# One searched instruction order replaced by another in a retention and channel-mix kernel

## The chip, the cores and the metric

One core of one Trainium2 chip. The metric is device time in microseconds of the one launch. A second number, the span, is the time from the first to the last instruction of one profiled execution.

## The reference

Two steps. First a retention recurrence over 4 sequences of 768 tokens, 8 heads of 64: `state = gamma[h] * state + k_t v_t^T`, and `y_t = q_t state / 8`. Then a channel mix on its output x (512 wide), with x' the row of the token before:

```
xk = mu_k * x + (1 - mu_k) * x'
xr = mu_r * x + (1 - mu_r) * x'
k  = relu(xk @ w_k)              # 512 -> 1024
v  = (k * k) @ w_v               # 1024 -> 512
out = sigmoid(xr @ w_r) * v
```

## The kernel before

The tokens are cut into 12 blocks of 256 (three for each sequence, numbered n = 0 to 11). Every step of every block is a word in one long string, `ORDER`. A loop at the end of the kernel takes the words one after another and issues their instructions; `@` gives the PSUM banks that the word's result takes, `~` the engine where there is a choice (v DVE, a ACT, p POOL, s SP). Each engine runs its own words in the order in which they stand; waits between engines follow from who reads and writes what, PSUM taken by whole banks. Nothing else schedules the program. The words:

- `lq lk lv` load q, k and v of a block (POOL); `tq tk` are transposing loads on SP's queue for blocks 9 to 11; `st`, `sc` store (SP). Rings of 4 buffers mean that a load of block n waits for the last reader of block n-4.
- `vs.n` scales v by the decay (DVE, L280). `Tq Tk` transpose q and k on PE, `Eq Ek` copy them out of PSUM (ACT, L265).
- `S` scores (PE, L375 to L396), `M` masks them (DVE, L420). `C` the block's state (PE, L432 to L461), `U` adds it to the carried state (DVE or ACT, L485), `G` decays that.
- The block's output gathers in a pair of banks named "I": `I.n` (`inter_off`) adds the carried state's part for one row half, `Y.n` (`intra`) the part from inside the block, and for blocks 2 to 5 `J.n` (`inter_on`) the carried state's part for the other row half (L507); for the other blocks `Y.n` holds this part too. `D.n` (`yout`, DVE, L573 or L580) writes it out as x, `dx.n` takes the difference to the token before (L595).
- `X.n.w.j` mixes (DVE, L621), w 0 for the keys and 1 for the gate. `K.n.g` keys (PE, L635 or L645), `Qa` Relu and `Qb` Square (ACT, L667 and L675 or L679), `R.n.t` the gate (PE, L688), `s` its Sigmoid (ACT, L694), `V.n.t.h` the half h of the values of 128 tokens (PE, L700), `Vc` the same by halves of the columns (L718), `O`, `Oc` the result (DVE, L706, L725).
- `z.c` multiplies zeros on PE, as a filler (L774, L781); `gy`, `mu`, `mt`, `me`, `wk`, `wr`, `wv` set up constants and weights.

Blocks 3 and 4, 6 and 7, 9 and 10 share one set of keys. In the order of before all two-bank results stand on neighbouring banks (01, 23, 45 or 67).

Of the kernel before, what the change touches and what calls it, by code (L numbers as in the profile page):

```python
# [28 lines left out]
KP = ()  # L29
DT = (9, 10, 11)  # L30
ORDER = """
gy.0 lq.0.0.2~s lk.0.0.2~s mu~s cq.0.0.2~a lv.0~p z.8@7 Tq.0.0.2@0 ck.0.0.2~a vs.0~v Eq.0.0.2~a
z.3@1 Tk.0.0.2@1 Ek.0.0.2~a z.3@2 S.0.0.0.2@23 lk.0.2.4~p S.0.1.0.2@45 M.0.1.0.2~v Tk.0.2.4@1
gy.1~a Ek.0.2.4~a lq.0.2.4~p C.0@67 Tq.0.2.4@0 Eq.0.2.4~a U.0.0~v lv.1~p lk.1~p M.0.0.0.2~v
U.0.1 z.3@4 S.0.1.2.4@45 M.0.1.2.4~v I.0@01 mt@2 me lq.1~p S.0.0.2.4@67 M.0.0.2.4~v lq.2~p G.0~a
vs.1~v z.4@3 Y.0 Tk.1@6 Ek.1~a D.0~v dx.0~v z.3@3 Tq.1@7 X.0.0.0 Eq.1~a X.0.1.1 wk.1~p C.1@23
U.1.0 lk.2~p z.4@4 S.1.1@45 M.1.1~v z.1@0 I.1@01 wk.0~p S.1.0@67 M.1.0~v X.0.0.3 Tq.2@4 Eq.2~a
z.2@5 Y.1 lv.2~p X.0.0.1 X.0.0.2 z.1@5 K.0.2@4 Tk.2@5 D.1~v X.0.1.0 dx.1~v Qa.0.2 X.0.1.2
X.1.0.0 Ek.2~a K.0.3@0 Qa.0.3 Qb.0.3 X.1.0.2 X.1.0.1 S.2.1@67 K.0.0@5 Qa.0.0 K.0.1@0 X.1.0.3
K.1.2@1 K.1.0@5 Qb.0.0 wr~p X.1.1.0 Qa.0.1 U.1.1 G.1~a vs.2~v X.0.1.3 Qa.1.0 Qa.1.2 Qb.0.1  # L40
X.1.1.1 C.2@0 U.2.0 K.1.1@3 Qa.1.1 I.2@45 lv.3~p M.2.1~v S.2.0@01 K.1.3@2 lq.3~p Qb.1.2 R.0.1@3
Qa.1.3 lk.3~p M.2.0~v X.1.1.2 Y.2 lk.4~p lq.4~p Qb.1.3 s.0.1 lv.4~p X.1.1.3 vs.3~v J.2 D.2~v
R.1.0@2 R.1.1@3 Qb.1.1 s.1.0 Tq.3@2 s.1.1 Eq.3~a C.3@67 Tk.3@4 Ek.3~a R.0.0@3 s.0.0 Tk.4@2
# [42 lines left out]
def kernel(  # L86
# [210 lines left out]
    def trans(a):
        def go(e, n, j0=0, j1=NJ):
            src = held_as(n, a)
            pt = turned(n, a, j0, j1)  # L300
            for j in range(j0, j1):
                for i in range(2):
                    if quarters(n, a):
                        for u in range(2):
                            for s, h, hp in heads(j):
                                nc.tensor.transpose(  # L306
                                    pt[low(s), u, j - j0, i], src[low(u), i, h], ident[low(u), low(u)]
                                )
                        continue
# [209 lines left out]
    def inter_on(e, n):  # L519
        inter(n, 0)  # L520

    def intra_half(n):
        py = pairs(banks("I", n))
        for j in range(NJ):
            for i in range(2):
                for u in range(2):
                    for a, h, hp in heads(j):
                        nc.tensor.matmul(
                            py[low(hp), u, j, i * W : i * W + W],
                            lhsT=VS(n)[low(u), i, h],  # L530
                            rhs=a_half(n)[low(u), a, j, i, :],
                            start=False, stop=False, skip_group_check=True,
                        )
        inter(n, 0)
# [31 lines left out]

    def yout(e, n, u=None):
        x, c = col(n)
        if half(n):
            x = x[:, :, c : c + TM].rearrange("p j (i u t) -> p j i u t", i=2, u=2)  # L570
            g = gy.rearrange("p j (i u t) -> p j i u t", i=2, u=2)
# [95 lines left out]
        nc.scalar.activation(out=kr, in_=banks("K", n, g, *u), func=AF.Relu)  # L667
# [143 lines left out]
    def load_wv(e, h):  # L811
# [62 lines left out]
```

## Time and profile before

| | |
|---|---|
| time, median of 3 runs | 154.3 us (154.3 to 154.64) |
| span of the profiled execution | 152.4 us |
| time less span, taken as what lies around the span | 1.9 us |
| PE busy | 145.3 us |
| DVE busy | 128.0 us |
| ACT busy | 94.5 us |
| granted TensorE clock | 1.00 |

Of the profiled execution only the span is known; its own time is taken to be the median, and the 1.9 us to be the same before and after. PE is TensorE's products, PEld its weight loads, DVE VectorE, ACT ScalarE, POOL GpSimd and SP SyncE. A line of the chain or the timeline gives start, length, engine, line and operation, and how many instructions were merged. Consecutive instructions of an engine overlap a little, so the distance between two starts is less than the length. An end of a product is modelled, and lies up to 0.17 us behind the start of the next.

### The profile page before, as it was taken

How to read it: one execution, taken by the hardware profiler on the slowest of the kernel's cores; microseconds unless marked ns; L12 is line 12 of the kernel's file. 1: busy time of each engine (PE TensorE's matmuls, PEld its weight loads, DVE VectorE, ACT ScalarE, POOL GpSimd, SP SyncE). 2: the span in 40 equal slices, each digit the busy share in tenths (PEclk: the TensorE clock that was granted, in tenths of full speed). 3: DMA queues.
4: the chain of work that ended last, by engine and by line, in shares of the span. 5: the costliest groups of instructions: out<-in, count | busy, mean ns of one | idle time of the engine just before them, and what ended most of it. 6: DMA issues, size and time to landing. Idle time of an engine off the chain costs nothing.

```text
span 152.4 us, 4956 instructions
## 1 busy us (share of the span) xinstructions
PE 145.3 (95%) x2129; PEld 82.4 (54%) x2129; DVE 128.0 (84%) x204; ACT 94.5 (62%) x172; POOL 62.1 (41%) x77
## 2 busy tenths in 40 slices
PE   7969899999999999999999999999999999999991
PEld 3345467657864545545448544447664444466460
DVE  2289999999999999999999998998999999331651
ACT  3655259979955679966418807869450089739430
POOL 7965658999746920599989000000000000000000
PEclk9999999999999999999999999999999999999999
DMA  5999999999999999299999999928103013003153
GB/s 146 237 241 192 181 240 237 148 148 223 167 178 216 213 225 286 68 239 166 258 188 238 236 168 126 152 89 109 38 4 138 0 71 142 0 0 138 69 207 138
DMA packets 56525, 23.83 MB, mean 156 GB/s; under 512 B 48056, under 2 KB 52024, under 8 KB 56504
## 3 DMA queue, kind: packets, MB, share of 16 engines
q0 software_dynamic: 45200, 14.95, 82.1%
q1 hardware_dynamic: 10872, 8.26, 22.3%
q8 instruction: 16, 0.26, 0.7%
q10 hardware_dynamic: 432, 0.32, 0.7%
q14 instruction: 5, 0.04, 0.1%
HBM read 24.31 MB, written 6.29 MB: 201 GB/s over the span
## 4 chain that ended last, share of the span: by engine, by line
PE 73%; DVE 11%; DMA 11%; issue 2%; ACT 0%; DVEq 0%; POOLq 0%
PE ps L700 24%; PE ps L688 14%; PE ps L635 12%; PE ps L645 11%; DMA kT<-k 6%; DMA v<-in_v_dram 5%; DVE a L420 3%; PE ps L507 2%; PE ps L311 2%; DVE xk L621 2%; DVE xT L580 2%; DVE dx L595 2%; PE ps L544 1%; DVE vs L280 1%; PE ps L388 1%
## 5 line engine op out<-in xcount | busy, mean ns | idle before, releaser
L700 PE MATMUL ps<-wv,k2s 128*128 128x512 f16 x184 | 43.9, 380 | 0.0
L667 ACT ACTIVATE kr<-ps 128x512 f32<-128x512 f32 x48 | 27.9, 594 | 23.0 <-PE ps L635 14.9
L700 PEld LDWEIGHTS <-k2s 128*128 128x128 f16 x184 | 17.2, 98 | 19.0
L706 DVE SCALAR_TENSOR_TENSOR os<-ps,rs 128x512 f32<-128x512 f32 x23 | 15.2, 684 | 12.1 <-PE ps L700 6.5
L688 PE MATMUL ps<-wr,xr 128*128 128x512 f16 x96 | 24.0, 379 | 0.0
L259 POOL DMA_DIRECT2D v<-in_v_dram x20 | 18.0, 911 | 13.6 <-DVE vs L280 8.3
L645 PE MATMUL ps<-xk,wk 128*128 128x256 f16 x192 | 23.4, 273 | 0.0
L635 PE MATMUL ps<-xk,wk 128*128 128x512 f16 x96 | 22.8, 379 | 0.0
L420 DVE TENSOR_TENSOR a<-ps,c_sb 128x1024 f16<-128x1024 f32 (+1 forms) x20 | 21.9, 1110 | 0.0
L694 ACT ACTIVATE rs<-ps 128x512 f32<-128x512 f32 x24 | 14.3, 594 | 10.6 <-PE ps L688 8.8
L645 PEld LDWEIGHTS <-wk 128*128 128x128 f16 x192 | 18.2, 98 | 3.9
L621 DVE SCALAR_TENSOR_TENSOR xr<-dx,mu,xT 128x256 f16<-128x256 f32 (+1 forms) x36 | 19.3, 566 | 0.0
L621 DVE SCALAR_TENSOR_TENSOR xk<-dx,mu,xT 128x256 f16<-128x256 f32 (+1 forms) x36 | 18.9, 569 | 0.3
L259 POOL DMA_DIRECT2D k<-in_k_dram x20 | 17.7, 896 | 3.5 <-DMA wv<-in_moe_w_v_dram 1.6
L280 DVE TENSOR_TENSOR vs<-v,csm_sb 128x1024 f16<-128x1024 f32 x12 | 14.5, 1217 | 3.3 <-DMA v<-in_v_dram 3.3
L675 ACT ACTIVATE k2s<-kr 128x512 f16<-128x512 f32 x24 | 14.7, 626 | 0.4
L595 DVE TENSOR_TENSOR dx<-xT 128x1024 f32<-128x1024 f32 x12 | 14.6, 1221 | 0.2
L635 PEld LDWEIGHTS <-wk 128*128 128x128 f16 x96 | 9.1, 98 | 10.5 <-issue 0.2
L679 ACT ACTIVATE k2s<-kr 128x512 f16<-128x512 f32 x24 | 14.5, 625 | 0.3
L688 PEld LDWEIGHTS <-xr 128*128 128x128 f16 x96 | 9.0, 98 | 10.0
L265 ACT COPY qT<-ps 128x1024 f16<-128x1024 f16 (+1 forms) x10 | 9.2, 924 | 7.7 <-PE ps L317 3.7
L265 ACT COPY kT<-ps 128x1024 f16<-128x1024 f16 (+1 forms) x10 | 9.3, 934 | 6.9 <-PE ps L306 3.4
(73 smaller groups left out, 151.3 us busy)
## 6 DMA issues: line engine op xcount, KB each, us to landing
out_dram<-os SPq DMA_DIRECT2D x23, 256.0 KB, 3.8
v<-in_v_dram POOLq DMA_DIRECT2D x20, 256.0 KB, 6.8
k<-in_k_dram POOLq DMA_DIRECT2D x21, 128.0 KB, 6.9
q<-in_q_dram POOLq DMA_DIRECT2D x13, 128.0 KB, 7.1
q<-in_q_dram POOLq DMA_DIRECT2D x5, 256.0 KB, 9.0
v<-in_v_dram POOLq DMA_DIRECT2D x2, 512.0 KB, 7.3
wv<-in_moe_w_v_dram POOLq DMA_DIRECT2D x2, 512.0 KB, 9.5
wk<-in_moe_w_k_dram POOLq DMA_DIRECT2D x2, 256.0 KB, 9.6
```

Of the source, the lines that this page charges most:

```text
L259: e.dma_start(out=to[:, i, hs], in_=src[:, i])
L265: e.copy(out=out, in_=in_)
L280: e.tensor_tensor(out=VS(n), in0=V32(n).rearrange("p (h i d) -> p i h d", i=2, h=H), in1=gks[:, int(half(n) or wide(n)), :, :, None].to_br ...
L420: nc.vector.tensor_tensor(out=dst, in0=dst if n in SPLITM else src, in1=mask[:, None, None, :].to_broadcast(list(dst.shape)), op=ALU.mult,)
L595: e.tensor_tensor(out=DX(k)[:, :, m * TM + t0 : m * TM + t1], in0=x[:, :, c + t0 : c + t1], in1=x[:, :, c - 1 + t0 : c - 1 + t1], op=ALU.s ...
L621: nc.vector.scalar_tensor_tensor(out=XM[w](k)[:, j, t0:t1], in0=DX(k)[:, j, t0:t1], scalar=mu[:, w * NCO + j : w * NCO + j + 1], in1=x[:, ...
L635: nc.tensor.matmul(banks("K", n, g), lhsT=wk16[:, co, g * P : g * P + P], rhs=XM[0](k)[:, co, :], start=(co == 0), stop=(co == NCO - 1),)
L645: nc.tensor.matmul(pz[:, i, :], lhsT=wk16[:, co, fo * P : fo * P + P], rhs=XM[0](k)[:, co, m * TM + t0 : m * TM + t1], start=(i == 0 and c ...
L667: nc.scalar.activation(out=kr, in_=banks("K", n, g, *u), func=AF.Relu)
L688: nc.tensor.matmul(banks("R", n, tb), lhsT=XM[1](k)[:, co, t : t + P], rhs=wr16[:, co, :], start=(co == 0), stop=(co == NCO - 1),)
L700: nc.tensor.matmul(banks("V", n, tb), lhsT=K2(n)[:, fo, tb * P : tb * P + P], rhs=wv16[:, fo, :], start=(fo == 0), stop=(fo == NFO - 1),)
L706: nc.vector.scalar_tensor_tensor(out=OS(2 * n + tb), in0=banks("V", n, tb), scalar=1.0 / (KSC * KSC), in1=RS(2 * n + tb), op0=ALU.mult, op ...
```

## The change

`ORDER` is replaced as a whole: the order of nearly all words behind the first dozen, and many banks. By count, the words are the same but for two things. One filler, `z.1@5` between `Y.1` and `K.0.2`, is gone. And there are ten new words `sy.2` to `sy.11`, each a small copy on ACT out of the banks "I". Words for other variants are added to the code and not used in the order (`ce`, `tu`, blocks in `QS`, a Square on POOL). The load lists on POOL are the same to `lq.6`, then in another order; SP's list of stores and transposing loads changes too.

```diff
+    seen_y = const.tile([P, 2, NJ], F32, name="seen_y")
+
+    def settle(e, n):
+        if wide(n):
+            u = slice(1 if first(n) else 0, 2)
+            copy(e, seen_y[:, u], banks("I", n)[:, u, 0 : NJ * C : C])
+        else:
+            copy(e, seen_y[low(0), 0, 0:2], banks("I", n)[low(0), 0, NJ * C - 2 :])
...
+        "sy": settle, "ce": load_late, "tu": scaled_eye, "Vc": values_c, "Oc": result_c, "sc": store_c,
```

The order from `C.1` to `J.5`, of before:

```
X.0.0.0 Eq.1~a X.0.1.1 wk.1~p C.1@23
U.1.0 lk.2~p z.4@4 S.1.1@45 M.1.1~v z.1@0 I.1@01 wk.0~p S.1.0@67 M.1.0~v X.0.0.3 Tq.2@4 Eq.2~a
z.2@5 Y.1 lv.2~p X.0.0.1 X.0.0.2 z.1@5 K.0.2@4 Tk.2@5 D.1~v X.0.1.0 dx.1~v Qa.0.2 X.0.1.2
X.1.0.0 Ek.2~a K.0.3@0 Qa.0.3 Qb.0.3 X.1.0.2 X.1.0.1 S.2.1@67 K.0.0@5 Qa.0.0 K.0.1@0 X.1.0.3
K.1.2@1 K.1.0@5 Qb.0.0 wr~p X.1.1.0 Qa.0.1 U.1.1 G.1~a vs.2~v X.0.1.3 Qa.1.0 Qa.1.2 Qb.0.1
X.1.1.1 C.2@0 U.2.0 K.1.1@3 Qa.1.1 I.2@45 lv.3~p M.2.1~v S.2.0@01 K.1.3@2 lq.3~p Qb.1.2 R.0.1@3
Qa.1.3 lk.3~p M.2.0~v X.1.1.2 Y.2 lk.4~p lq.4~p Qb.1.3 s.0.1 lv.4~p X.1.1.3 vs.3~v J.2 D.2~v
...
K.3.0@4 Qa.3.0 lk.7~p K.3.7@6 S.6@23 Qb.3.2 M.6~v I.5@01 Y.5 vs.6~v V.2.1.0@7
R.2.1@2 lv.10~p Qb.2.2 Qa.3.7 K.3.4@6 st.0.0 vs.7~v Qb.3.7 s.2.1 st.0.1 V.2.1.1 Tk.7@45 Qb.3.5
Qa.3.4 X.3.1.3 X.3.1.1 Qb.3.0 C.6@23 st.1.0 J.5
```

and of after:

```
z.2@7 Y.1 X.0.0.2 X.0.0.1 Tk.2@6 D.1~v K.0.2@7 Ek.2~a K.0.3@2 U.1.1 Qa.0.2~a dx.1~v lv.3~p
S.2.1@67 Qa.0.3~a S.2.0@01 X.0.1.3 K.0.0@4 G.1~a X.1.0.0 X.1.0.3 lq.3~p K.0.1@5 X.1.0.1 X.1.0.2
X.0.1.2 Qa.0.1~a K.1.3@2 X.1.1.1 Qa.0.0~a X.0.1.0 K.1.2@3 Qb.0.2~a M.2.0 lk.3~p K.1.0@4 Qa.1.2~a
vs.2~v Qb.0.3~a K.1.1@5 lk.4~p Qa.1.3~a X.1.1.2 C.2@3 Qb.0.1~a X.1.1.0 R.0.0@2 M.2.1 Qb.1.3~a
lq.4~p Qa.1.1~a R.0.1@0 U.2.0~v Qa.1.0~a vs.3~v s.0.0 I.2@67 Y.2 sy.2~a lv.4~p s.0.1 J.2
...
Qa.2.2~a lv.5~p K.2.1@2 vs.4~v Qa.2.0~a Qb.2.2~a S.4.1@01 X.2.1.0 S.4.0@45 I.3@67 Qa.2.1~a M.4.1
Y.3 sy.3~a Qb.1.0~a C.4@23 Qb.2.1~a J.3 V.1.1.0@0 D.3~v Qb.2.3~a V.0.0.0@1 G.3~a lq.6~p X.2.1.1
M.4.0 V.1.0.0@6 V.0.1.0@7 U.4.0~v X.2.1.2 lv.7~p V.1.1.1 U.4.1 dx.3~v I.4@23 Y.4 sy.4~a O.1.1 J.4
Tq.7@45 D.4~v V.0.1.1 Eq.7~a lk.7~p Tk.5@0 G.4~a dx.4~v R.2.0@4 lv.6~p Qb.2.0~a Tq.5@5 X.3.0.3
...
lk.6~p K.3.6@0 Qb.3.4~a O.2.0 Qa.3.0~a X.3.1.1 S.5.1@23 Qa.3.3~a S.5.0@67 M.5.1 C.5@5 lq.9~p
Qa.3.1~a V.2.1.0@4 Qa.3.6~a U.5.0~v V.2.1.1 Qb.3.6~a M.5.0 Qb.3.3~a Tk.7@01 I.5@23 O.2.1 Y.5
Ek.7~a sy.5~a J.5 st.2.1 Tk.8@45 st.1.1 D.5~v Tq.6@67 Qb.3.0~a st.2.0 K.3.5@0 st.1.0 Qb.3.1~a
Ek.8~a R.4.0@1 dx.5~v R.4.1@2 Eq.6~a X.5.0.1 vs.8~v Qa.3.5~a Tk.6@45 C.6@67 Ek.6~a R.3.0@0 lk.10~p
X.5.1.3 X.5.0.0 V.3.1.0@3 s.3.0 X.5.0.2 X.5.1.1 U.6.0~a R.3.1@4 Qb.3.5~a X.5.0.3 lq.8~p U.6.1
K.5.2@0 U.6.2 s.3.1 lv.11~p U.6.3 s.4.1 S.6@45 X.5.1.2 I.6@67 s.4.0 K.5.0@2 M.6 sy.6~a Qa.5.2~a
lk.9~p G.6~a S.7@01 X.5.1.0 Y.6 M.7 C.7@45 tq.9~s V.3.1.1 lq.11~p U.7.0~v V.3.0.0@0 U.7.1 O.3.1
K.5.1@1 D.6~v lq.10~p st.3.1 K.5.3@3 O.3.0 ...
```

and later, around `sy.11`:

```
X.9.1.1 K.9.7@4 O.7.1 K.9.4@6 X.9.1.0 st.7.1 K.9.5@2 X.9.1.2 Qa.9.4~a X.9.1.3 Qa.9.0~a I.11@01
K.9.6@6 Qb.9.4~a sy.11~a Qb.9.0~a Y.11 Qa.9.6~a K.9.2@7 D.11~v Qb.9.1~a s.8.1 R.10.1@6 Qa.9.2~a
dx.11~v R.10.0@3 Qa.9.5~a K.9.3@2 X.11.0.0
```

More of the change, by code (lines that the diff above doesn't have):

```diff
@@ L16 @@
 KUP = 4.0
+QDN = 64.0
 HALF = (6, 7, 8, 9, 10, 11)
@@ L22 @@
 WIDE = (2, 3, 4, 5)
+QS = ()
 PARTED = ()
@@ L38 @@
[L38 to L43, printed above, removed]
@@ new lines @@
+K.5.1@1 D.6~v lq.10~p st.3.1 K.5.3@3 U.7.2 V.3.0.1 Qa.5.3~a lv.10~p U.7.3 Qa.5.1~a V.4.1.0@6 G.7~v
+O.3.0 Qa.5.0~a Qb.5.1~a dx.6~v I.7@45 st.3.0 C.8@01 sy.7~a lk.11~p Tq.8@23 Qb.5.3~a tk.9~s Y.7
+Qb.5.0~a V.4.1.1 D.7~v Eq.8~a V.5.0.0@7 Qb.5.2~a O.4.1 V.5.1.0@4 dx.7~v V.5.1.1 U.8.0~v V.4.0.0@6
+X.6.0.3 X.6.1.0 R.5.0@5 X.6.0.0 V.4.0.1 s.5.0 X.6.0.2 V.5.0.1 U.8.1 X.6.0.1 R.5.1@5 X.6.1.1
+K.6.0@2 U.8.2 s.5.1 vs.10~v K.6.2@3 O.5.1 K.6.5@5 Qa.6.2~a X.6.1.2 st.5.1 Qa.6.0~a K.6.4@4 st.4.1
+O.5.0 Qb.6.2~a tq.10~s Qa.6.5~a O.4.0 S.8@23 I.8@01 Qa.6.4~a K.6.1@7 M.8 sy.8~a st.4.0 K.6.3@6
@@ new lines @@
+R.9.1@0 X.11.0.2 Qa.9.7~a O.8.1 K.11.2@2 Qb.9.3~a X.11.1.1 Qb.9.7~a X.11.1.3 K.11.3@1 X.11.1.2
+Qa.11.2~a R.11.1@5 Qa.11.3~a s.9.1 K.11.0@2 Qb.9.6~a K.11.1@4 Qb.9.2~a V.9.0.0@0 Qa.11.1~a
+Qa.11.0~a R.11.0@1 s.10.1 V.10.0.0@2 s.9.0 Qb.11.2~a V.9.1.0@4 s.10.0 V.9.0.1 V.10.1.0@3 O.9.0
+V.10.1.1 s.11.0 st.9.0 st.8.1 Qb.11.0~a V.9.1.1 Qb.11.3~a V.10.0.1 Qb.11.1~a O.9.1 V.11.0.0@1
+s.11.1 st.9.1 O.10.0 V.11.0.1 O.10.1 Vc.11.1.0@0 st.10.1 O.11.0 st.10.0 Vc.11.1.1@3 st.11.0
+Oc.11.1.0 sc.11.1.0~s Oc.11.1.1 sc.11.1.1~a
@@ L138 @@
     ).astype(np.float32)
+    gq_np = gam[None, None, :] ** (toks[0][:, :, None] + 1 - TM) / QDN
+    late_np = np.concatenate(
+        [gq_np.reshape(P, -1), np.tile(np.eye(W), (2, 1))], axis=1
+    ).astype(np.float32)
+    lated = nc.inline_tensor(late_np, name="late")
     c16d = nc.inline_tensor(c16_np, name="c16")
@@ L172 @@
     mu = const.tile([P, 2 * NCO], F32, name="mu")
+    late = mu8[:, 0 : 2 * H + W]
+    turn = A2(0)[:, 2 * H * W :].rearrange("p (i h t) -> p i h t", i=2, h=H)
     nu = const.tile([P, 2 * NCO], F32, name="nu")
@@ L286, in quarters, with scaled, load_late, scaled_eye @@
         return half(n) and n not in PAIR[a]
+    def scaled(n, a):
+        return a == 0 and n in QS
+    def load_late(e):
+        e.dma_start(out=late, in_=lated.ap())
+    def scaled_eye(e, h0, h1):
+        hs = slice(h0, h1)
+        gq = late[:, 0 : 2 * H].rearrange("p (i h) -> p i h", i=2)
+        to = [P, 2, h1 - h0, W]
+        e.tensor_tensor(
+            out=turn[:, :, hs], in0=late[:, None, None, 2 * H :].to_broadcast(to),
+            in1=gq[:, :, hs, None].to_broadcast(to), op=ALU.mult,
+        )
     def turned(n, a, j0, j1):
+        if scaled(n, a):
+            pt = banks("T", n, a, j0)
+            return pt.rearrange("c u (j i p) -> c u j i p", j=NJ, i=2)[:, :, j0:j1]
         pt = banks("T", n, a, j0).bitcast(F16)
@@ L305, in go @@
                             for s, h, hp in heads(j):
+                                if scaled(n, a):
+                                    nc.tensor.matmul(
+                                        pt[low(s), u, j - j0, i], lhsT=src[low(u), i, h],
+                                        rhs=turn[low(u), i, h], start=(j == j0 and i == 0),
+                                        stop=(j == j1 - 1 and i == 1), skip_group_check=True,
+                                    )
+                                    continue
                                 nc.tensor.transpose(
@@ L568, in yout @@
         x, c = col(n)
+        if n in QS:
+            x = x[:, :, c : c + TM].rearrange("p j (i u t) -> p u j i t", i=2, u=2)
+            y = banks("I", n).rearrange("p u (j i t) -> p u j i t", j=NJ, i=2)
+            for v in range(2):
+                if e is nc.scalar:
+                    e.activation(
+                        out=x[:, v], in_=y[:, v], func=AF.Copy, scale=0.125 * KSC / KUP * QDN
+                    )
+                else:
+                    e.tensor_scalar(
+                        out=x[:, v], in0=y[:, v], scalar1=0.125 * KSC / KUP * QDN, scalar2=None,
+                        op0=ALU.mult,
+                    )
+            return
         if half(n):
@@ L669, in squared @@
     def squared(e, n, g, *u):
+        if e is nc.gpsimd:
+            kr = held.pop((n, g, u))
+            idle.append(kr)
+            to = k2s[:, n % 3 : n % 3 + 2, g, :] if joint(n) else K2(n)[:, 2 * g : 2 * g + 2]
+            e.tensor_tensor(out=to, in0=kr, in1=kr, op=ALU.mult)
+            return
         w = 4 if u else 2
```

68 lines of the change are left out of this document (23 added, 45 removed).

## The prediction

> **What bounds the kernel now.** I read the page first, then the table of the span by stretches, then the waits of TensorE, then the chain of waits.
>
> ```profile
> span 152.4 us, 4956 instructions
> PE 145.3 (95%) x2129; PEld 82.4 (54%) x2129; DVE 128.0 (84%) x204; ACT 94.5 (62%) x172; POOL 62.1 (41%) x77
> DVE  2289999999999999999999998998999999331651
> ...
> 60.00:80.00 20.00, 20.00 (x336) 9.91 (x332) 19.66 (x32) 11.99 (x24) 16.51 (x19) 1.00 1.38 189
> 80.00:100.00 20.00, 19.57 (x358) 11.45 (x357) 18.93 (x28) 13.75 (x25) 3.77 (x5) 1.00 1.54 191
> 100.00:120.00 20.00, 20.00 (x352) 11.53 (x351) 19.08 (x31) 9.34 (x17) 0.00 (x0) 1.00 0.27 55
> ...
> PE ps L375 <- DMA kT<-k: 0.4, 1, 0.4
> PE ps L450 <- DVE vs L280: 0.2, 1, 0.2
> ...
> 147.29 1.76 PE ps L718 x16
> 149.07 0.42 DVE os L725
> ```
>
> The columns of the stretches are start and end, length, then PE, PEld, DVE and ACT busy. From 28 us on PE runs without a break but for the two waits listed: 0.2 for `C.2` on `vs.2` and 0.4 for `S.10` on a transposed load. DVE is nearly as full (19.66 of 20) until 120 us; ACT is used two thirds. So the end is set by the list of PE: a change of order is worth what it takes from or adds to PE's waits, and DVE has little room to catch up after a delay. The last product ends at 149.05, and one result step and a store follow to 152.4. The profiled span is 1.9 below the median of 154.3; I add that distance to every sum.
>
> **What PE's list costs.** I split it into large steps (K, R, V, Vc: keys, gate, values) and small ones (scores, states, transposes).
>
> ```profile
> 64.93 0.97 PE ps L688 x4
> ...
> 73.55 0.86 PE ps L700 x4
> ...
> 113.71 7.01 PE ps L700 x32
> ```
>
> In the chain, four products of 512 columns take 0.86 behind a large step and 0.97 behind a small one; eight such steps in a row take 7.01, one switch included, so 0.865 each and 0.11 for the switch. Counted in the two lists, the large steps are the same 120, and so are the small ones, save one filler, `z.1@5`. But the switches from a small to a large step behind the first key step fall from 28 to 20: eight fewer are 0.9 us off PE.
>
> [...]
>
> **The head.** Up to `Y.1` both lists give PE, ACT and DVE the same work; the other banks add no wait there, since each earlier reader is one that the step waits for anyway or is done by then (`Tk.0.0.2` now waits for `Eq.0.0.2`, hidden under `z.3`). Then:
>
> ```profile
> 20.56 0.39 PE L781 MATMUL ps<-zero 128*128 128x512 f16 x1
> 20.78 1.09 PE L645 MATMUL ps<-xk,wk 128*128 128x256 f16 x8
> 21.80 0.64 PE L317 MATMUL ps<-c_sb,k 128*64 128x128 f16 x16
> 22.39 1.03 PE L645 MATMUL ps<-xk,wk 128*128 128x256 f16 x8
> ...
> 21.11 1.23 DVE L580 TENSOR_TENSOR xT<-ps,gy_sb 128x1024 f32<-128x1024 f32 x1
> ...
> 22.64 1.22 DVE L595 TENSOR_TENSOR dx<-xT 128x1024 f32<-128x1024 f32 x1
> ...
> 24.18 1.67 DVE L621 SCALAR_TENSOR_TENSOR xk<-dx,mu,xT 128x256 f16<-128x256 f32 x4
> 26.15 0.42 DVE L485 TENSOR_TENSOR t<-ps,tg 128x256 f32<-128x256 f32 x1
> 26.49 1.22 DVE L280 TENSOR_TENSOR vs<-v,csm_sb 128x1024 f16<-128x1024 f32 x1
> ...
> 82.69 2.51 SPq L351 DMA_TRANSPOSE qT<-q  x1
> 85.26 0.69 SPq L713 DMA_DIRECT2D out_dram<-os  x1
> ...
> DMA to landing us min/median/max: 4.3/7.5/9.2
> ```
>
> Before, `Y.1` was followed by the filler, `K.0.2` (held back by its last X, the step in front of `D.1` at 21.11), `Tk.2`, and `K.0.3` at 22.39. Now `Tk.2` stands in that hole, from 20.5 to 21.05, and `K.0.3` starts at 21.8: 0.6 earlier. The old waits of `C.2` (0.2) and `S.10` (0.4) go. The second is the less sure: on SP's queue `tk.10` now follows `st.5.1`, `st.4.1`, `tq.10` and `st.4.0`, at most 2.51 + 3 x 0.69 = 4.6 of issuing. `st.5.1` waits for `O.5.1`, which also frees the bank for `K.6.4`; from there PE has 11 large, six small steps and three switches to `S.10`, 11.9. So `tk.10` is issued 7.3 us ahead or more; the three loads into kT landed 4.3 to 9.2 us after issue (the last row). I take no wait, from the median of 7.5 and the issues nearer 4; at the longest landing it would be 1.9 late. Gains in all: 0.9 + 0.6 + 0.2 + 0.4 = 2.1.
>
> Against it: a DVE step begins 0.08 before the one ahead of it ends (26.15 + 0.42 against 26.49), so start to start D, dx, vs (and M) cost 1.14, U 0.34, X 0.40. From `D.1` at 21.11 come `U.1.1`, `dx.1` and four X, then `X.1.0.2` ends at 25.8. PE, with `K.0.3`, two S (0.55), `K.0.0` and `K.0.1`, reaches the third product of `K.1.3`, which needs it, at 25.3: 0.5. Then three more X, `M.2.0`, `vs.2` to 29.25, where PE is at 29.05: `C.2` waits 0.25. `U.2.0` ends at 31.5 and PE is at `I.2` at 31.35: 0.15. Sum 0.9.
>
> **The settles.** The words say that operations are kept; the code adds ten ACT copies `sy`, each reading a PSUM bank between two passes that add into it. For blocks 2 to 5, `sy` waits for `Y` and `J` waits for `sy`; for 6 to 11, `sy` waits for `I` and `Y` for `sy`. Before has no such copy; the nearest rows are a trip from PE over ACT back to PE in the head, and the smallest ACT copy:
>
> ```profile
> 6.42 0.41 PE L317 MATMUL ps<-c_sb,k 128*64 128x128 f16 x8
> 6.88 0.59 ACT L265 COPY kT<-ps 128x512 f16<-128x512 f16 x1 [0.74 <-PE ps L317]
> 7.52 0.42 PE L396 MATMUL ps<-qT,kT 64*64 64x128 f16 x16
> 11.65 0.17 ACT L767 COPY mu<-ps 128x8 f32<-128x8 f32 x1 [0.66 <-PE ps L764]
> ...
> 31.39 0.64 PE L544 MATMUL ps<-a,vs 128*64 128x128 f16 x16
> 31.96 0.31 PE L507 MATMUL ps<-qT,tg 64*64 64x128 f16 x8
> 32.20 1.04 PE L688 MATMUL ps<-wr,xr 128*128 128x512 f16 x4
> ...
> 34.55 0.37 PE ps L450 x16
> ...
> 57.41 1.01 ACT L265 COPY qT<-ps 128x1024 f16<-128x1024 f16 x1
> 58.30 1.03 ACT L265 COPY kT<-ps 128x1024 f16<-128x1024 f16 x1
> 59.21 0.65 ACT L675 ACTIVATE k2s<-kr 128x512 f16<-128x512 f32 x1
> 84.05 1.57 ACT L667 ACTIVATE kr<-ps 128x512 f32<-128x512 f32 x3 [0.49 <-PE ps L645]
> ...
> 135.83 1.29 DVE L706 SCALAR_TENSOR_TENSOR os<-ps,rs 128x512 f32<-128x512 f32 x2 [4.92 <-ACT rs L694]
> ```
>
> `Y.2` takes 0.57 and `J.2` 0.24 to the next start; `J.2` starts at 31.96 while `Y.2` drains until 32.03 (0.07). The trip is 0.05 out, 0.17 for the copy, 0.05 back: a bare settle costs 0.34 when PE has nothing between, from nothing (other PE work covers it) to over 1 (the copy stands behind ACT's queue). Case by case:
> - `J.2` and `J.4` stand right behind `Y`, and ACT has caught up by then (the three Relu steps in 1.57 are 0.49 apart; from `K.0.2` to `sy.2` ACT has some 8 us of steps and PE 11): 0.34 each.
> - `J.3` has `C.4` between and waits nothing. But `Qb.1.0` stands behind `sy.3` on ACT, and `V.1.1.0` needs it: `Y.3`'s end + 0.05 + 0.17 + 0.63 + 0.05 = 0.90 against PE's 0.37 (`C.4`, as the row at 34.55) + 0.14 (`J.3`, an estimate: half of `J.2` and a little) = 0.51: 0.39.
> - `sy.5` stands behind `Ek.7`. From the end of `Tk.7`, ACT needs 0.05 + 1.01 + 0.17 + 0.05 = 1.28; PE gets there after `I.5` and `Y.5`, 0.24 + 0.57 = 0.81: `J.5` waits 0.47. With it waits `D.5`, and all behind it on DVE: from the end of `M.5.0` it is 0.57 + 0.47 + 0.31 to the end of `J.5`, and DVE has one result step (0.60) in between, so it idles 0.75.
> - From block 6 on, 0.5 to 1.7 us of PE steps stand between `I` and `Y`, and ACT is at most one step behind: nothing. If a long step is in front, 0.5 each.
>
> Sum 1.54. At six later places (`K.2.1`, `S.7`, `K.6.4`, `K.8.1`, `K.8.0`, `K.9.1`) a step follows within 0.1 of the DVE or ACT step that frees its bank or input: 0.05 each, 0.3 (bounds 0 and 1.5).
>
> **The sum.** Gains 2.1, waits 0.9 + 1.54 + 0.3 = 2.7: PE's end is 0.6 to 0.8 later (2.7 less 2.1; 0.8 when I carry the switch at 0.10, with which the list of before adds up to its own 128.1). I take 0.8: span 153.2, time 155.1. The tail is the same: a half product, one result step, one store.
>
> **The rivals.**
> *The order wins (faster).* If `Ek.7` is started early enough, or `Y.5` late enough, that `J.5` waits under 0.1, and `Qb.1.0` is done when `V.1.1.0` comes, then DVE keeps its lead, and only the head's waits and the two bare settles stay: 0.5 to 0.9 + 0.68, so 1.2 to 1.6 against 2.1: 0.4 to 0.9 faster, 153.4 at best. It decides at `D.5`, from a wait of DVE there under 0.3 instead of the 0.75. For it: DVE is full, so it may reach `M.5.0` later than I say. Against it: `sy.5` is behind a step of 1.01 in any case. Chance 0.20.
> *ACT's queue becomes the bound.* ACT's steps then cost their whole durations (0.60, 0.63, 1.01) and not the 0.49 to 0.9 between starts. `K.2.3` waits for `Ek.4` 0.3, `K.2.1` for `Qa.2.3` behind `Eq.4` 0.5 more, `J.5` 0.3 more, and behind `sy.11` come `R.10.1`, `R.10.0` and `K.9.3`, whose banks `Qa.9.6`, `s.8.1` and `Qa.9.5` free: 0.3 each. That is 2.0 more: 157.1. For it: from `K.9.1` to `V.9.0.0` ACT has ten Relu, eight Square, two Sigmoid and a settle, 12.4 us at whole durations; against it: PE has 18 large steps there, 15.6. Chance 0.15.
> *A load comes late.* On POOL's queue `lq.8` now stands behind `lk.10`, which waits for `C.6`. From `C.6` to `Tq.8` PE has 11 large steps (9.5), seven small ones of 0.24 to 0.43 (like the row at 34.55; 2.4) and four switches (0.4): 12.3 us. The two issues of `lk.10` take 1.8, and landings of q at that time took:
>
> ```profile
> L259 POOL DMA_DIRECT2D q<-in_q_dram x6: 896/919/982, 72.3 to 82.8; - x6
> ...
> DMA to landing us min/median/max: 7.1/9.7/13.1
> ```
>
> The median leaves 0.8, the maximum is 2.6 late: 157.7. Chance 0.10.
> *Level.* The 2.1 and the 2.7 cancel; the forecast's own uncertainty, since each is a sum of small terms. Chance 0.15.
>
> **How the numbers follow.** The forecast (155.1, its own range 154.7 to 156.0) has 0.40. 0.3% is 0.46 us, about what a measurement of this kernel can tell from no change. Faster: 0.20. Same: the level case and the low edge of the forecast, 0.20. Slower: the rest of the forecast, ACT's queue, the load, 0.60. The range runs from 153.3 (just under the best of the faster rival) to 157.2 (just over ACT's queue), and leaves out the load and some of each edge.
>
> **What would show it.** Right: PE's waits list ACT (`seen_y`) at L507 three times, 0.3 to 0.5 each, and none on kT; large steps behind small ones number eight fewer; PE's last product ends near 149.9; `D.5` starts some 0.8 after DVE is free. Wrong: the waits of PE on `seen_y` near nothing and an end before 149 (the order wins); waits of PE on Relu or qT/kT copies of 0.3 and more (ACT); a wait of `Tq.8` on q (the load); a granted clock under 1.00 anywhere.

## The result, and the profile after

The changed kernel takes 158.46 us in the median (157.08 to 159.22 over four executions) against 154.3: a ratio of 1.026, with an interval of 1.020 to 1.031. It is slower, and slower by far more than the 155.1 that was forecast; 158.46 lies outside the range. The profiled execution is the fastest of the four, 157.08 with a span of 155.3, so its trace shows 2.9 us (155.3 less 152.4) of the 4.2 lost in the median. The ratios here and below are to the kernel before, run beside each kernel, and leave out executions that lie over 1.5% above the fastest of their kernel; the medians hold all of them.

The page, the span by stretches, TensorE's waits and the first and last rows of the end of the chain, of the changed kernel (columns as before):

```profile
span 155.3 us, 4963 instructions
PE 145.3 (94%) x2128; PEld 83.2 (54%) x2128; DVE 127.8 (82%) x204; ACT 92.7 (60%) x182; POOL 62.1 (40%) x77
...
60.00:80.00 20.00, 19.56 (x444) 11.51 (x443) 18.78 (x29) 15.76 (x31) 13.76 (x17) 1.00 1.25 186
80.00:100.00 20.00, 18.06 (x249) 9.10 (x246) 17.18 (x27) 9.16 (x18) 5.02 (x6) 1.00 1.65 168
100.00:120.00 20.00, 20.00 (x444) 12.06 (x443) 19.44 (x32) 12.78 (x26) 0.00 (x0) 1.00 0.53 100
...
PE ps L695 <- DVE os L772: 1.5, 1, 1.5
...
PE ps L544 <- ACT seen_y L276: 1.0, 3, 0.4
...
PE ps L766 <- issue: 0.4, 1, 0.4
PE ps L766 <- ACT k2s L745: 0.2, 1, 0.2
...
150.28 1.76 PE ps L784 x16
...
152.07 0.42 DVE os L791
```

PE's busy time is 145.3 as before, to the tenth: the 0.9 of saved switches does not show in the sum. About half of the loss is in one stretch: from 80 to 100 us PE is busy 18.06 of 20 and DVE 17.18, where before had 19.57 and 18.93. One wait stands out, 1.5 us of PE on a result step of DVE (`os`), which the forecast did not have. The settles are where it put them: three waits on `seen_y`, 1.0 together, and one of 0.2 on a Square. One more, of 0.4, is marked "issue": the profile names nothing that PE waited for (the last section comes back to it).

The big wait, followed backwards through the timelines of PE, DVE and POOL of the changed kernel:

```profile
92.56 2.75 PE L695 MATMUL ps<-xk,wk 128*128 128x512 f16 x12
96.86 1.02 PE L695 MATMUL ps<-xk,wk 128*128 128x512 f16 x4 [1.55 <-DVE os L772]
...
92.16 0.41 DVE L522 TENSOR_TENSOR tg<-ps,tg 128x256 f16<-128x256 f32 x1
94.98 1.23 DVE L291 TENSOR_TENSOR vs<-v,csm_sb 128x1024 f16<-128x1024 f32 x1 [2.40 <-DMA v<-in_v_dram]
96.12 0.68 DVE L772 SCALAR_TENSOR_TENSOR os<-ps,rs 128x512 f32<-128x512 f32 x1
...
63.76 1.80 POOL L270 DMA_DIRECT2D q<-in_q_dram  x2
71.81 1.76 POOL L270 DMA_DIRECT2D k<-in_k_dram  x2 [6.24 <-PE ps L469]
73.53 0.90 POOL L265 DMA_DIRECT2D q<-in_q_dram  x1
74.40 1.81 POOL L270 DMA_DIRECT2D v<-in_v_dram  x2
76.16 1.82 POOL L270 DMA_DIRECT2D k<-in_k_dram  x2
77.90 3.58 POOL L270 DMA_DIRECT2D q<-in_q_dram  x4
81.36 1.89 POOL L270 DMA_DIRECT2D v<-in_v_dram  x2
...
DMA to landing us min/median/max: 12.7/12.7/12.7
```

Read from the top: `K.6.4` waits 1.55 for `O.5.1`, which frees its bank. `O.5.1` is a short step, but on DVE it stands behind `vs.10`, and `vs.10` waits 2.40 for the load `lv.10`. On POOL `lv.10` is the 12th and 13th issue of a row that begins with the two of `lk.10`, and `lk.10` waits 6.24 for `C.6`. At 0.87 an issue, 71.81 + 11 x 0.87 = 81.4, which is where it is issued. It then takes 12.7 to land (the last row, of the two pieces of `lv.10`).

### The profile page after: what moved, and what is told of

Read it like the earlier page. It is cut to its first block, busy times and chain, and to the rows that moved or that the text cites. A ratio compares the mean times of both kernels' runs of the same rounds, so it can differ in the third digit from the quotient of the medians.

```text
span 155.3 us, 4963 instructions
## 1 busy us (share of the span) xinstructions
PE 145.3 (94%) x2128; PEld 83.2 (54%) x2128; DVE 127.8 (82%) x204; ACT 92.7 (60%) x182; POOL 62.1 (40%) x77
## 4 chain that ended last, share of the span: by engine, by line
PE 45%; DVE 20%; DMA 16%; POOL 8%; issue 6%; ACT 2%; DVEq 0%; POOLq 0%; ACTq 0%
PE ps L766 15%; DMA v<-in_v_dram 13%; PE ps L695 8%; PE ps L705 7%; PE ps L754 7%; DVE xk L681 4%; DVE a L457 4%; POOL v L270 3%; DMA k<-in_k_dram 3%; DVE dx L655 3%; DVE xT L640 3%; DVE vs L291 2%; POOL k L270 2%; POOL q L270 2%; PE ps L544 2%
## 5 line engine op out<-in xcount | busy, mean ns | idle before, releaser
L766 PE MATMUL ps<-wv,k2s 128*128 128x512 f16 x184 | 42.4, 379 | 0.6 <-issue 0.4
L727 ACT ACTIVATE kr<-ps 128x512 f32<-128x512 f32 x48 | 27.4, 601 | 22.3 <-PE ps L695 12.3
L754 PE MATMUL ps<-wr,xr 128*128 128x512 f16 x96 | 23.5, 379 | 0.0
L760 ACT ACTIVATE rs<-ps 128x512 f32<-128x512 f32 x24 | 13.7, 601 | 15.2 <-PE ps L754 9.0
L695 PEld LDWEIGHTS <-wk 128*128 128x128 f16 x96 | 9.0, 98 | 12.1 <-issue 1.8
L741 ACT ACTIVATE k2s<-kr 128x512 f16<-128x512 f32 x24 | 14.3, 630 | 0.2
L745 ACT ACTIVATE k2s<-kr 128x512 f16<-128x512 f32 x24 | 14.2, 629 | 0.0
```

What stands on the lines that cost most here:

```text
L695: nc.tensor.matmul(banks("K", n, g), lhsT=wk16[:, co, g * P : g * P + P], rhs=XM[0](k)[:, co, :], start=(co == 0), stop=(co == NCO - 1),)
L754: nc.tensor.matmul(banks("R", n, tb), lhsT=XM[1](k)[:, co, t : t + P], rhs=wr16[:, co, :], start=(co == 0), stop=(co == NCO - 1),)
L766: nc.tensor.matmul(banks("V", n, tb), lhsT=K2(n)[:, fo, tb * P : tb * P + P], rhs=wv16[:, fo, :], start=(fo == 0), stop=(fo == NFO - 1),)
```

## The experiments

Twelve kernels were run. The first group asks what makes `lv.10` late, the second what the settles cost, the third how the late load reaches PE and what is left. The diffs show the words of `ORDER` that move.

**The load moved ahead of the wait.**

```diff
-... C.6@67 Ek.6~a R.3.0@0 lk.10~p
+... C.6@67 Ek.6~a R.3.0@0 lv.10~p lk.10~p
```

> The changed kernel with one load moved: on POOL's queue lv.10 stands in front of lk.10 instead of six loads behind it, so it doesn't stand behind lk.10's wait for C.6. Queue theory (the load of V 10 comes late because its issue stands behind that wait): lv.10 is issued near 65 us instead of 81.4, vs.10 waits at most 0.3 us for it (2.4 in the changed kernel's profile), PE's 1.5 us before the K step at 96.9 goes, and the median is 155.3 to 156.0 against 158.5 (1.5 of the profiled run, which was the fastest, and what the median runs lie above it). Settle theory (the small waits at the order's changes carry the loss, and the late load only takes up a wait that would come anyway behind it): vs.10 is in time, but K.6.4 waits for DVE as before or the next product does, and the median stays above 157.5.

Measured: 155.26 (155.1 to 157.41), a ratio of 1.005 (1.0032 to 1.0067). DVE's waits on loads of v, first of the changed kernel, then of this one:

```profile
DVE vs L291 <- DMA v<-in_v_dram: 5.8, 2, 3.4
```

```profile
DVE vs L290 <- DMA v<-in_v_dram: 3.5, 1, 3.5
```

The 3.4 or 3.5 is `vs.0` in the head, which waits in every kernel here; the 2.4 of `vs.10` is gone, and PE's wait at `K.6.4` with it. The queue theory's number holds (155.26, at the lower edge of its 155.3 to 156.0), and the settle theory (above 157.5) falls: most of the loss hangs on one load.

**The transposing load moved behind the place.**

```diff
-lk.11~p Tq.8@23 Qb.5.3~a tk.9~s Y.7
+lk.11~p Tq.8@23 Qb.5.3~a Y.7
...
-X.6.1.2 st.5.1 Qa.6.0~a
+X.6.1.2 st.5.1 tk.9~s Qa.6.0~a
```

> The changed kernel with one transposing load moved: tk.9 on SP's queue goes behind st.5.1, so that it is not in flight while lv.10 is. Theory of the transposing load (landings jumped from 88.0 to 93.3 us while tk.9 was in flight; it holds up the other loads by some 5 us): lv.10 lands at 90 to 91 instead of 94.0 to 94.9, vs.10 no longer waits, and PE's 1.5 us before the K step at 96.9 goes; S.9 may then wait up to 2 us for tk.9, so the median is 156.5 to 158.5. Queue theory (lv.10 was issued too late, behind lk.10's wait): lv.10 still lands at 93 or later, vs.10 still waits 1.5 us or more, K.6.4 still waits for it, and S.9's wait for tk.9 is added: 158.5 to 160.5.

Measured: 154.67 (154.12 to 156.08), a ratio of 1.0013 (0.9985 to 1.004), better than either theory said. The rows for v between 80 and 97 us:

```profile
  DMA v<-in_v_dram: 0.8, 1
...
DMA to landing us min/median/max: 10.9/11.0/11.1
```

`lv.10` is issued where it was and lands 1.7 sooner after its issue. `vs.10` still waits 0.8, but PE does not feel that much, and `S.9` did not wait for the later `tk.9`. One landing proves little, however: in the six profiles of this document whose loads and transposing loads stand as in the change, `lv.10` took 9.8 to 12.8, and in the three with `tk.9` moved 9.9 to 11.0. The next kernel is the clearer test.

**Both transposing loads of block 9 moved there.**

```diff
-C.7@45 tq.9~s V.3.1.1
+C.7@45 V.3.1.1
...
-X.6.1.2 st.5.1 Qa.6.0~a
+X.6.1.2 st.5.1 tq.9~s tk.9~s Qa.6.0~a
```

> The changed kernel with both transposing loads of chunk 9, tq.9 and tk.9, behind st.5.1 on SP's queue, so that none is in flight from 77 to 95 us. Theory that transposing loads hold up the others: the loads issued from 77 to 85 us, which took 8.4 to 12.8 us in the changed kernel, take 5 to 7 us, lv.10 lands by 88.5, and vs.10 doesn't wait; the median is 154.0 to 155.0, or up to 2 more if S.9 now waits for tq.9. Theory that the loads only wait for each other (a row of 14 of them issued 0.87 us apart): they still take 8 us or more, lv.10 lands at 90 or later.

Measured: 155.56 (155.51 to 155.76), a ratio of 1.0097 (1.0083 to 1.011). The four issues of q between 77 and 84 us, from issue to landing, in the changed kernel and then in this one, and the wait that took the place:

```profile
DMA to landing us min/median/max: 8.4/8.4/12.8
```

```profile
DMA to landing us min/median/max: 6.0/6.8/6.8
...
99.17 0.45 PE L412 MATMUL ps<-qT,kT 64*64 64x64 f16 x32 [1.12 <-DMA kT<-k]
```

Without a transposing load in flight the same loads land in 6.0 to 6.8, and `lv.10` in 7.5 to 7.7 instead of 12.7. That confirms the theory of the transposing loads, and `vs.10` does not wait. So being behind the wait (the first kernel) and being slowed in flight (this one) both had to happen; taking away either is enough. The time is worse than with `tk.9` moved alone because `S.9` now waits 1.12 for it.

**The waiting load moved behind the others.**

```diff
-... R.3.0@0 lk.10~p
+... R.3.0@0
...
-V.3.0.1 Qa.5.3~a lv.10~p U.7.3
+V.3.0.1 Qa.5.3~a lv.10~p lk.10~p U.7.3
```

> The changed kernel with the one load that waits, lk.10, moved behind lv.10 on POOL's queue; nothing else on that queue is moved and no transposing load is. Queue theory: with the wait for C.6 no longer in front of them, lq.8 to lv.10 are issued from about 66 us on, lv.10 by 75 or 76 instead of 81.4, all in time; vs.10 doesn't wait, the median is 154.5 to 155.4. Theory that tk.9 alone is to blame: lv.10 is in time too, but then tk.9 holds up lk.10 and lk.11 (landing 93 or later), which nobody needs before 99, so the time is the same and the two differ only in where the jump in the landings lies. Rival: SP's queue or another load becomes late in their stead, 156 or more.

Measured: 157.39 (156.08 to 159.75), a ratio of 1.0187 (1.0158 to 1.0216). The rival held. `vs.10` is in time, but the loads now run in one dense row from 62 us, and PE stops elsewhere:

```profile
71.40 0.41 PE L469 MATMUL ps<-vs,k 64*64 64x64 f16 x28 [0.64 <-issue]
...
78.15 0.22 PE L412 MATMUL ps<-qT,kT 64*64 64x64 f16 x4 [0.94 <-issue]
```

Both stops lie inside a group of 32 products that read the same inputs, behind the fourth and behind the 28th; the profile names nothing that PE waited for. The profiled execution (156.08) is the fastest of six; where the longer ones lose more is not known.

**The changed kernel once more, beside the edits.**

> The changed kernel once more, unedited, beside the three edits of this group, so that they have it on the same chip. If what the earlier edits gained is the late load, it measures 157.0 to 159.2 as before, 2.5 to 4 above the edit that moved tk.9 (154.7). If that gain was in truth a difference between chips, it measures 154.5 to 156.0 here and its load of V 10 is in time.

Measured: 156.11 (155.79 to 159.14), a ratio of 1.0118 (1.0102 to 1.0134); three executions at 155.8 to 156.1 with the clock at 1.00, two at 158.13 and 159.14 with a mean clock of 0.989. With the four of the first result that makes nine, four of them at 0.989. So the expectation hit neither case: the changed kernel has no single time, it spreads over 3.4 us, and what an edit to it gains depends on how many of the long ones fall into a group. The clock is not all of the spread: the longest of the nine, 159.22, had a clock of 1.00. The profile shows the same wait as above, 1.4 at `K.6.4`, and `lv.10` takes 12.1 to land. So the load was late here too, and the gain of the edits is not merely a difference between chips; whether a part of the 158.5 is one stays open. `lv.10` is in time when it lands within 11.2 of its issue (81.4 to 92.6), and the 9.8 to 12.8 seen lie on both sides of that; this may be another part of the spread, but was not tested.

**Two neighbours on ACT exchanged, loads untouched.**

```diff
-Y.3 sy.3~a Qb.1.0~a
+Y.3 Qb.1.0~a sy.3~a
...
-Ek.7~a sy.5~a J.5
+sy.5~a Ek.7~a J.5
```

> The changed kernel with two neighbours on ACT exchanged at two places: Qb.1.0 ahead of sy.3, and sy.5 ahead of Ek.7; the loads are as they were. Prediction's term: V.1.1.0 no longer waits for the Square (0.23 us) and J.5's wait falls from 0.38 to 0.2 or less, D.5 starts up to 0.3 earlier. If the small waits add up one for one, the median falls by 0.5 to 0.7 (158.5 to 157.9). Queue theory: C.6, and with it lk.10 and lv.10, move earlier by the same half microsecond, so most of it is kept: 157.9 to 158.3. Theory that the late load sets the place whatever comes before it: the wait of vs.10 grows by what was saved, and the median stays at 158.3 to 158.7.

Measured: 156.0 (153.65 to 158.6 over twelve executions), a ratio of 1.0011 (0.9979 to 1.0042). All theories miss, since they started from 158.5; on the median nothing can be told. What it gave is a profile of one of the long executions (157.71). TensorE's timeline and the stretches around its `K.6.4` (the columns as above; the 1.00, 0.79, 0.50 and 0.86 are the granted clock):

```profile
96.15 1.02 PE L695 MATMUL ps<-xk,wk 128*128 128x512 f16 x4 [2.19 <-DVE os L772]
...
97.88 3.21 PE L695 MATMUL ps<-xk,wk 128*128 128x512 f16 x8
...
94.00:96.00 2.00, 0.00 (x0) 0.00 (x0) 1.73 (x2) 1.29 (x3) 0.00 (x0) 1.00 1.08 73
96.00:98.00 2.00, 1.85 (x53) 1.12 (x53) 2.00 (x5) 0.60 (x1) 0.00 (x0) 0.79 0.53 193
98.00:100.00 2.00, 2.00 (x6) 0.63 (x6) 2.00 (x2) 0.29 (x2) 0.00 (x0) 0.50 1.08 255
100.00:102.00 2.00, 2.00 (x116) 1.27 (x114) 1.17 (x3) 1.87 (x4) 0.00 (x0) 0.86 0.92 208
102.00:104.00 2.00, 2.00 (x32) 0.96 (x19) 1.90 (x4) 1.42 (x4) 0.00 (x0) 1.00 1.07 73
```

Here the wait is 2.19, and behind it the clock falls to half: eight products take 3.21 in place of the 1.90 that the same eight take with `vs.10` moved (below). The clock lost over the three stretches is (0.21 + 0.50 + 0.14) x 2 = 1.7 us. A mean clock of 0.989 over some 155 us is a loss of 1.7 too, so the four executions of the changed kernel at 0.989 would fit the same event. None of those four was profiled, and the clock can drop at other places too (the last section).

**`vs.10` moved behind three result steps, no load touched.**

```diff
-K.6.0@2 U.8.2 s.5.1 vs.10~v K.6.2@3 O.5.1
+K.6.0@2 U.8.2 s.5.1 K.6.2@3 O.5.1
...
-Qa.6.5~a O.4.0 S.8@23
+Qa.6.5~a O.4.0 vs.10~v S.8@23
```

> The changed kernel with one DVE instruction moved and no load: vs.10 goes behind O.4.0, three evictions later; the loads and the transposing loads are as they were. Theory that the late load reaches PE through DVE's queue: lv.10 still lands at 93 to 95 us, but O.5.1 no longer stands behind vs.10, K.6.4's wait (1.4 to 2.2 us) goes, no stretch of half clock follows, and the median is 154.3 to 155.0 with a spread under 1 us. Rival, the load itself or the traffic around it holds PE up (PE's own wait on issue, or the next load's reader): PE loses 1 us or more near 90 to 100 us all the same, and the median stays at 155.8 or above.

Measured: 154.87 (154.2 to 156.65), a ratio of 1.0036 (1.0016 to 1.0057), every execution at a clock of 0.996 or more. DVE and PE in the same place:

```profile
92.89 0.69 DVE L772 SCALAR_TENSOR_TENSOR os<-ps,rs 128x512 f32<-128x512 f32 x1 [0.26 <-ACT rs L760]
...
95.35 1.22 DVE L291 TENSOR_TENSOR vs<-v,csm_sb 128x1024 f16<-128x1024 f32 x1
...
92.06 3.62 PE L695 MATMUL ps<-xk,wk 128*128 128x512 f16 x16
```

The four key steps run on in 3.62 with no wait. In this profile `lv.10` landed at 92.1, in time even for the old place, so the profile alone does not test the order. But in the kernel with both cures (below) it takes 12.4 to 93.8, and `vs.10` starts at 95.0 without a wait, so the order on DVE is what keeps the load from PE. This is the cause, shown from the other side: with the lists of loads untouched, the loss of 2.0 (156.11 beside 154.11) to 4.2 us (158.46 beside 154.3) shrinks to 0.6 (154.87 beside 154.26). One execution still took 156.65 at a clock of 1.00, so a spread of under 1 us, as expected, did not come.

**The settles alone, in the order of before:** `sy.n` in front of `J.n` for blocks 2 to 5 and in front of `Y.n` for 6 to 11.

```diff
+        "sy": settle,
...
-... J.2 D.2~v
+... sy.2~a J.2 D.2~v
```

> The kernel before in its own order and with its own loads, with the ten small ACT copies added (sy.n right in front of J.n for n of 2 to 5, in front of Y.n for n of 6 to 11). It measures those copies alone. Prediction's term: 0.26 to 0.4 us for each of J.2, J.3, J.4 and J.5 where PE had no other work between, nothing for the other six, so 0.8 to 1.5 in all, median 155.1 to 155.8 against 154.3. Rival: the copies lie beside slack that before had at those places (its DVE waits in the same stretch), and it stays within 0.4 of 154.3. Other rival: Y.n on DVE or ACT's queue is held up, and it costs over 2 us.

Measured: 160.61 (159.92 to 162.24), a ratio of 1.042 (1.038 to 1.047): 6.2 us slower, the other rival. TensorE's waits:

```profile
PE ps L571 <- ACT seen_y L273: 5.6, 6, 2.2
...
PE ps L541 <- ACT seen_y L273: 0.5, 1, 0.5
```

Of these 6.1 us of waits on the copies, 5.6 is on the six blocks for which I had forecast no wait, up to 2.2 at one of them. There the copy stands on ACT behind whatever its queue holds, and `Y.n` behind `I.n` with less work between. (The profiled execution is the longest, 162.24: the clock fell behind the wait of 2.2, as the last section says.) In the changed order the same six cost nothing: their cost belongs to the order, not to the copy.

**The exchanges, with `tk.9` out of the way** (the edits of those two kernels, in one).

> The changed kernel with tk.9 behind st.5.1 and the two exchanges on ACT (Qb.1.0 ahead of sy.3, sy.5 ahead of Ek.7). With the late load out of the way the small waits should count one for one: V.1.1.0's 0.23, 0.12 of J.5's and 0.2 to 0.3 of D.5's. Prediction's theory: 153.9 to 154.2, that is 0.5 to 0.8 below the edit with tk.9 alone (154.67). Rival, the small waits are taken up by slack further on: 154.5 to 154.8.

Measured: 154.31 (153.97 to 158.35), a ratio of 1.0015 (0.9998 to 1.0031), against 1.0013 with `tk.9` alone. No gain can be told.

**The half steps covered by transpose groups,** on top of that.

```diff
-J.2 X.1.1.3 Tq.3@2
+X.1.1.3 Tq.3@2 J.2
...
-Y.4 sy.4~a O.1.1 J.4 Tq.7@45
+Y.4 sy.4~a O.1.1 Tq.7@45 J.4
...
-J.5 st.2.1 Tk.8@45
+st.2.1 Tk.8@45 J.5
```

> The changed kernel with tk.9 behind st.5.1, the two exchanges on ACT, and each waiting half step moved behind a transpose group that stood right after it: J.2 behind Tq.3, J.4 behind Tq.7, J.5 behind Tk.8, so that PE works while ACT copies. Prediction's theory (a settle costs what PE finds no work for): the three waits of 0.26 to 0.31 on ACT's copies go, PE gains 0.6 to 0.8, and the median is 153.5 to 153.9 against 154.31 without the three moves. Rival, D.2, D.4 and D.5 start later by the length of the transpose group less the wait, and DVE passes that on: 154.1 to 154.6.

Measured: 154.47 (154.02 to 155.33), a ratio of 1.0026 (1.0006 to 1.0046). The rival held. The three waits on `seen_y` are gone from TensorE's list, and two others have grown:

```profile
PE ps L705 <- DVE xk L681: 0.5, 1, 0.5
PE ps L695 <- ACT kT L276: 0.4, 1, 0.4
```

`D.2` starts later behind the transposes, so `K.2.3` waits longer for its X; and with `Ek.7` behind `sy.5`, `K.3.5` waits for the bank that `Ek.7` frees.

**Both cures together.** `vs.10` moved, the two exchanges, the three half steps covered.

> The changed kernel with vs.10 behind O.4.0, the two exchanges on ACT and the three half steps moved behind transpose groups; tk.9 stays where the change put it. If the late load and the settles are the whole loss and add up: 153.3 to 153.9, below the kernel before (154.1 to 154.45), the terms being 1.4 to 4 for the load and 1.0 to 1.4 for the settles below the changed kernel. If the settles' share is taken up by slack, 154.2 to 154.8.

Measured: 154.61 (153.99 to 155.4), a ratio of 1.0031 (1.001 to 1.0053): 0.3 below `vs.10` alone, which the two intervals do not tell apart. The case of the slack held.

**The best of the pieces.** `vs.10` moved, `sy.3` behind `Qb.1.0`, `J.4` behind `Tq.7`, `J.5` behind `Tk.8`, the rest as in the change.

```diff
-Y.3 sy.3~a Qb.1.0~a
+Y.3 Qb.1.0~a sy.3~a
...
-J.4 Tq.7@45
+Tq.7@45 J.4
...
-Ek.7~a sy.5~a J.5 st.2.1 Tk.8@45
+Ek.7~a sy.5~a st.2.1 Tk.8@45 J.5
...
-Qa.6.5~a O.4.0 S.8@23
+Qa.6.5~a O.4.0 vs.10~v S.8@23
```

> The changed kernel with vs.10 behind O.4.0 and three of the small waits covered in another way: sy.3 behind Qb.1.0, J.4 behind Tq.7, J.5 behind Tk.8 with Ek.7 left ahead of sy.5; J.2 stays where the change put it, since moving it behind Tq.3 only shifted its wait to K.2.3 (0.18 to 0.35 and 0.54 us), and sy.5 stays behind Ek.7, since exchanging them only shifted the wait to K.3.5 (0.36). If the three waits (0.23, 0.31, 0.38 us) go and no new one takes their place, 0.9 less than with vs.10 moved alone (154.87): 153.8 to 154.2, level with or below the kernel before. If DVE passes the later starts of D.4 and D.5 on, 154.4 to 154.8.

Measured: 154.5 (153.67 to 156.32), a ratio of 1.0008 (0.998 to 1.0036). The three waits went and nothing took their place in the list:

```profile
PE ps L544 <- ACT seen_y L276: 0.3, 1, 0.3
PE ps L705 <- DVE xk L681: 0.2, 1, 0.2
```

From `K.0.3` on PE waits 0.95 where it waited 1.82 with `vs.10` moved alone. Only 0.42 of the 0.87 came off the way from there to the last product (127.07 against 127.49). So the best version from these pieces is level with the kernel before; none beat it.

## Why the prediction was wrong

The sign was right, and the sum of small terms described the kernel without its accident: `vs.10` moved alone gives 154.87, and its last product starts at 149.66 and ends at 149.9, against a forecast of 155.1 and an end near 149.9. ACT's queue did not become the bound either: after the head no wait of TensorE on a Relu or on a copy of qT or kT is in the list of the changed kernel. The size was not, by these steps:

- **"A load comes late", the step that failed.** The sum had no term for a load, and this rival had a chance of 0.10. It had the place, `lk.10` waiting for `C.6` in front of other loads. But it followed one load only, the next (`lq.8`), and that came in time (issued at 73.53; no wait of `Tq.8` in the list). The last load of the row, eleven issues of 0.87 later, was not followed to its reader: `lv.10`, issued at 81.4, wanted at 92.6 by DVE, so 11.2 to land. The rows that the rival itself quoted, 7.1 to 13.1 from issue to landing, lie on both sides of that, so it was a case to price. And the price of the rival was the wait alone. In the runs, with this load issued early the loss falls to 0.8 (155.26 beside 154.45).
- **What stands behind the waiting instruction.** The reader of the late load, `C.10`, is far off. It was DVE's order that made the wait PE's: `O.5.1` queued behind `vs.10`. `K.6.4` was among my six tight places, at 0.05 with a bound of 1.5 for all six; it alone took 1.4 and 1.55 in the two profiles of the changed kernel.
- **The clock.** "A granted clock under 1.00 anywhere" was listed as a sign of error and priced at nothing. In the profile where the wait reached 2.19 it added 1.7, which no term had.
- **The eight fewer switches, 0.9.** PE's busy time is 145.3 in both profiles. From `K.0.3` to the last product, waits left out, PE needs 125.6 us before and 125.7 to 126.1 in the profiles of the changed kernel, of `vs.10` moved alone and of the best version (start of the last product less start of `K.0.3` less all idle time between). Single steps did get cheaper where a switch went (`K.2.2` from 0.98 to 0.87, `V.1.0.0` from 0.97 to 0.86, start to start), but others grew (`Y.9` and `Y.10`, now in front of a large step, by 0.2 each, `Tq.4` by 0.17; `K.1.3` by up to 0.3, which is its X coming late and belongs to the head). A gain counted at one kind of border was lost in part at others that I had not counted; what made each of those dearer, and where the rest went, is open. The two steps named did fall by the 0.11 of the forecast, and the sum by nothing.
- **The settles, 1.54.** Measured 0.26 for `J.2`, 0.31 for `J.4`, 0.23 for `V.1.1.0`, 0.38 for `J.5`, 1.18 together, each somewhat smaller than forecast, and nothing from block 6 on, as said. `D.5` left DVE idle for 0.90 (0.75 forecast):

```profile
67.83 1.22 DVE L640 TENSOR_TENSOR xT<-ps,gy_sb 128x1024 f32<-128x1024 f32 x1 [0.90 <-PE ps L544]
```

  But three of these waits and part of that idle time, taken away, gave 0.4 at most: here a wait on PE's list was an upper bound of what its removal brought.
- **The head.** `K.0.3` starts 0.3 to 0.65 earlier (22.11 and 21.74 in the two profiles against 22.39; 0.6 forecast). `K.1.3` takes 1.05 to 1.19 in place of 0.89 (0.13 of it shown as a wait for its X), `I.2` waits 0.11, and `C.2` not at all: 0.3 to 0.4 where I had 0.9.
- **`S.10`** does not wait for its transposing load any more, as forecast.

Two errors in the small terms, 0.9 of gain that did not come and some 1.1 of loss that did not (settles, head and tight places, 2.7 forecast and 1.5 to 1.6 found), nearly cancelled; that 154.87 is close to 155.1 is partly luck.

## What to carry to other kernels

When loads are reordered behind one that waits, count every issue behind it and carry each load to its reader, the last one first; then look at what stands behind that reader on its engine, since that is who really waits. Behind the two waits of some 2 us on TensorE (2.19 and 2.25) the clock fell to about half and 1.7 us more were lost each time: a forecast with such a wait should carry that price too. Moving the reader of the late load down its engine's list was worth more than any of the small waits, and no run shows a cost of it.

## What the hardware showed that was not expected

- The clock fell to 0.50 after 2.19 us without work and was back at 1.00 by 102 us; after waits of 1.4 and 1.55 at the same place it stayed at 1.00. The fall cost 1.7 us. Two more profiles lost the same 1.7 elsewhere. With the settles in the order of before, the wait of 2.25 that ends at 128.8 is followed by a clock of 0.51 and 0.64 in the stretches from 130 to 134. With `lv.10` moved ahead, TensorE waited 1.20 and 0.38 in the head and was busy 0.70 of the 2 us from 8 to 10; the clock was 0.70, 0.50 and 0.95 in the next three stretches of 2 us. So a mean clock of 0.989 does not by itself point to `K.6.4`, and how much idle time it takes is open.
- With a transposing load in flight, ordinary loads issued by another engine took longer: 8.4 to 12.8 us from issue to landing with it, 6.0 to 6.8 without, for the same four loads.
- With the loads issued in one dense row, PE stopped in the middle of two groups of products for 0.64 and 0.94 us, with nothing named that it waited for. Five other profiles have such stops, of 0.3 to 0.6, among them the changed kernel's own (0.40, ending at 89.97). The packets in the traces say more: all eight stops end 1.2 to 1.44 us after a 16 KB packet on the queue that the profile calls "instruction" (q8) has ended, and these packets come 3 to 13 us apart. In the changed kernel it ran from 87.58 to 88.54. PE's instructions may have come late, but that is an estimate of mine from these times and was not shown: the traces of before and of the changed kernel hold 32 such packets, and one such stop. Whether the loads are to blame is open: the packet before the stop of 0.64 took 1.82, but the one before the 0.94 took 0.97, as many do. No run moved these packets.
- Ten copies of 0.14 to 0.17 us each (their times in the changed kernel) cost 6.2 us in the order of before; in the changed order PE's waits on them are 1.0 in all.
